# A spectral filter plus MLP on one core: the transform over d by half-sample cosines and sines

## The chip, the cores and the metric

The kernel runs on one core of a Trainium2 chip. A core has a matrix engine (TensorE, PE in the profile, with its weight loads as PEld), VectorE (DVE), ScalarE (ACT), GpSimd (POOL), SyncE (SP), which issues the DMAs here, and 16 DMA engines. The metric is device microseconds of one execution; the number given for a kernel is the median of several executions.

## What is computed

```python
xn = layernorm(x)                               # x: (1, 2048, 512), over the last axis
X  = rfft2(xn, axes=(-2, -1)) * (w_r + 1j*w_i)  # w: (2048, 257)
y  = irfft2(X, s=(2048, 512), axes=(-2, -1))
h  = xn @ w1 + b1                               # w1: (512, 1792)
out = x + y + (h * tanh(softplus(h))) @ w2      # w2: (1792, 512)
```

The two parts read the same normalised rows and are added. S = 2048 is the sequence, d = 512 the width.

## The kernel before, in words

Every matrix product is done in f16 with an operand split in a high and a low part: `mm3` (lines 59 to 65) issues three matmuls into one PSUM tile (high by high on line 61, high by low on line 64, low by high on line 65). Each result leaves PSUM as a new pair: ScalarE writes the high part, VectorE the low part (`split`, and lines such as 486 and 487).

**MLP.** For each of four groups of 512 rows and each of 14 blocks of 128 hidden units, `mlp_up` issues 12 matmuls into `ph`, ScalarE applies Mish into `hb`, and `split` makes the pair `a`; two blocks later `mlp_down` issues 12 matmuls into four accumulators `pa_0` to `pa_3`. These are all 128x512 matmuls, 1344 in all. A generator hands them out in half tiles of 12.

**Spectral part.** The sequence is written as 128 x 16, s = 16 s1 + s2.

- `s1_forward` (line 93): for each of 16 values of s2, three matmuls with the table cT against a row `xh` of 512 values of d, into `psS`; results go to DRAM (`d_y1`), to come back in another layout.
- `p2_unit` (line 332): the s2 transform, 16 tiles. d is cut in four quarters d2 of 128, and the 128x128 matrix `c_p2` acts on (part, s2, d2) at once: 16 s2 by 4 quarters by 2 parts. A tile `psP` is 12 matmuls 128 wide, and gives `z` with four planes k = 0..3.
- `spectrum` (line 358): once for each of four chunks c, the transform over the 128 values of d1 within a quarter, the weights, and the pair `u`. The even frequencies come first: `ere` and `eim` are six matmuls of 512 columns each, three for plane 0 and three for plane 1. ScalarE copies `eim` to `es`; VectorE forms four sums and differences X (lines 414 to 417), two products on VectorE and two on POOL with the weights `wE` (lines 421 to 424), two sums, four sums and differences back (lines 435 to 438), then the splits into planes 0 and 1 of `u`. For frequency 0 and the Nyquist column a row goes through `g0`, `r0`, `h0` by small DMAs, and in chunk 0 four columns are mended (lines 445 to 450). The odd frequencies follow: `ore` and `oim`, six matmuls each from planes 2 and 3, four products on VectorE straight from PSUM (lines 464 to 468), two sums on POOL, and the splits into planes 2 and 3 (the tiles `o` take the buffers of the `w`).
- `dp_unit` (line 476): the inverse over d1, 16 tiles `psA`. Planes 0 and 1 of `u` are added up into columns 0..255, planes 2 and 3 into 256..511: 12 matmuls of 256 columns. The pair `at` goes to DRAM (`d_a`).
- `ip_unit` (line 496): read back as `ai`, inverse over s2 with `c_ip2` into `psT`, pair `tt` to DRAM (`d_t`).
- `s1_inverse` (line 587): read back as `yi`, three matmuls of 512 columns into `psY`, added to the output rows.

**What sets the order.** `stream_a` (line 626) writes the spectral units for chunk c, those of chunk c - 1 and the pieces of `spectrum` between its `yield`s in turn, and the loop on line 699 lays MLP half tiles between them, up to half tile `B_END` = 100 in `N_UNITS` = 72 steps. A scheduler then sets the final order on each engine, and an engine works through its own list in that order. All spectral PSUM tiles share two buffers (`ps_f`, tag "f"); `u`, `z` and the `w` tiles have one buffer each.

Of the kernel before, what the change touches and what calls it, by code (L numbers as in the profile page):

```python
# [11 lines left out]
F16 = mybir.dt.float16  # L12
# [12 lines left out]
N_UNITS = 72  # L25
# [5 lines left out]
O_P2, O_IP2, O_DE, O_DO, O_IE, O_IO, O_ID = 0, 512, 1024, 2048, 3072, 4096, 5120  # L31
N_CM = 5120 + 128
# [3 lines left out]
def spectral_mlp_kernel(ctx, tc, x, wt, w0, w1, b1, w2, cT, cIT, cM, out):  # L36
# [36 lines left out]
    c_de = cMt[:, O_DE : O_DE + 1024].rearrange("p (e o h q) -> p e o h q", e=2, o=2, h=2)  # L73
    c_do = cMt[:, O_DO : O_DO + 1024].rearrange("p (e o h q) -> p e o h q", e=2, o=2, h=2)
    c_ie = cMt[:, O_IE : O_IE + 1024].rearrange("p (e h q) -> p e h q", e=2, h=2)
    c_io = cMt[:, O_IO : O_IO + 1024].rearrange("p (e h q) -> p e h q", e=2, h=2)
# [281 lines left out]
    def spectrum(c):  # L358
        s_u, c0t = sc["u"], sc["c0t"]
        z = zt[c]  # L360
        wEt, wOt = wts[c]
        u = tp.tile([P, 2, 4, 4, P], F16, tag="u", name=f"u_{c}")
        ut[c] = u

        def dmm(name, mat, k0, o):
            ps = ps_f.tile([P, 512], F32, tag="f", name=name)
            for e in range(2):
                mm3(
                    ps,
                    lambda h: mat[:, e, o, h, :],  # L370
                    lambda h: z[:, h, k0 + e].rearrange("p g q -> p (g q)"),
                    e == 0,
                    e == 1,
                    e == 0,
                )
            return ps

        def split_u(k, r):
            split(flat(u[:, 0, k]), flat(u[:, 1, k]), r, s_u)

        ere = dmm(f"ere_{c}", c_de, 0, 0)
        eim = dmm(f"eim_{c}", c_de, 0, 1)
        es = tp.tile([P, 512], F32, tag="xs", name=f"es_{c}", bufs=2)
        nc.scalar.copy(es, eim)

        er0 = tp.tile([1, 512], F32, tag="xs", name=f"er0_{c}", bufs=2)
        nc.scalar.copy(er0, ere[0:1, :])  # L387
        q0 = slice(32 * c, 32 * c + 4)
        g0 = sp.tile([P, 2, 2, 64], F32, tag="g0", name=f"g0_{c}")
        nc.sync.dma_start(  # L390
            g0[q0, 0].rearrange("g a q -> g (a q)"), er0.rearrange("p (g q) -> p g q", g=4)
        )
        nc.sync.dma_start(
# [62 lines left out]
        for h in range(2):  # L456
            for r in range(2):
                nc.sync.dma_start(u[0:1, h, r], h0[q0, h, r])
# [420 lines left out]
```

## Time and profile before

| | |
|---|---|
| median of 3 runs | 423.24 us (422.02 to 425.58) |
| profiled execution, first to last instruction | 424.4 us (no other time is recorded for it) |
| mean granted TensorE clock in it | 0.986 |
| busy: PE, PEld, DVE | 391.0, 194.1, 241.3 us |
| busy: ACT, POOL | 172.4, 42.2 us |
| matmuls | 2099 |
| DMA | 61.02 MB, mean 144 GB/s |

How to read the rows. A group has a line of the kernel, an engine, an operation, "out<-in" by the program's names, the shape and a count; behind the bar its busy time in us, the mean ns of one, and the idle time of the engine just before it with what ended it. A timeline row has its start and its length in us. A stretch has its length, then for PE, PEld, DVE, ACT and POOL the busy us with the number of instructions, then the granted clock, the busy share of the DMA engines and GB/s. In the chain of waits, each row is a piece of the work that ended last, followed back from the end.

### The profile page before, as it was taken

What the parts mean: (1) busy time and instruction counts of PE and PEld (TensorE: products, weight loads), DVE (VectorE), ACT (ScalarE), POOL (GpSimd) and SP (SyncE); (2) the same over time, 40 slices, a digit from 0 to 9 for tenths busy, and PEclk for the clock granted to TensorE, in tenths of its full rate; (3) what the DMA queues carried; (4) which work ended last, traced back from release to release, by engine and by line L of the source; (5) the groups of instructions that cost most, each with busy time, mean ns of one, the idle gap of its engine ahead of it and who ended that gap; (6) DMA issues with size and microseconds to landing.
All of it is one profiled execution on the core that took longest, in us unless ns stands there. A gap on an engine that the chain in (4) does not pass through costs nothing.

```text
span 424.4 us, 5542 instructions
## 1 busy us (share of the span) xinstructions
PE 391.0 (92%) x2099; PEld 194.1 (46%) x2099; DVE 241.3 (57%) x453; ACT 172.4 (41%) x261; POOL 42.2 (10%) x45
## 2 busy tenths in 40 slices
PE   0787899499899999989999999999999999999995
PEld 0433344244445455436554455554455544554442
DVE  5759899995455123773247943339625287332554
ACT  2896462442635324334343334333524243433110
POOL 0000102332040000220002020011200022000000
PEclk9999999889999999989999999999999999999999
DMA  7899882588154701032227214233024210233796
GB/s 247 268 345 330 272 259 91 159 256 269 53 160 114 233 25 51 0 99 71 81 76 239 85 49 123 76 127 124 2 74 151 74 51 25 76 127 126 219 296 247
DMA packets 48811, 61.02 MB, mean 144 GB/s; under 512 B 3168, under 2 KB 31360, under 8 KB 48528
## 3 DMA queue, kind: packets, MB, share of 16 engines
q1 hardware_dynamic: 48784, 60.67, 44.7%
q8 instruction: 16, 0.26, 0.2%
q14 instruction: 11, 0.09, 0.1%
HBM read 43.85 MB, written 16.78 MB: 143 GB/s over the span
## 4 chain that ended last, share of the span: by engine, by line
PE 72%; DVE 13%; DMA 6%; ACT 4%; issue 2%; POOL 0%; SPq 0%; DVEq 0%; ACTq 0%; POOLq 0%
PE pa L65 9%; PE pa L64 9%; PE pa L61 9%; PE ph L61 9%; PE ph L65 9%; PE ph L64 9%; DVE q L273 2%; DMA w1s<-in_w_dram 2%; PE pt L164 2%; ACT w1t L236 1%; PE psA L61 1%; PE psA L64 1%; PE psA L65 1%; DMA w2s<-in_w_dram 1%; DMA ai<-d_a 1%
## 5 line engine op out<-in xcount | busy, mean ns | idle before, releaser
L61 PE MATMUL ph<-xnT,w1t 128*128 128x512 f16 x224 | 85.2, 380 | 2.6 <-ACT hb L533 1.5
L533 ACT ACTIVATE hb<-ph,b1t,sc_exp 128x512 f32<-128x512 f32 x56 | 43.4, 775 | 107.4 <-PE ph L65 104.2
L65 PE MATMUL ph<-xnT,w1t 128*128 128x512 f16 x224 | 84.8, 379 | 2.4 <-DVE w1t L208 2.4
L61 PE MATMUL pa<-w2t,a 128*128 128x512 f16 x224 | 85.3, 383 | 1.6 <-ACT w2t L207 1.6
L64 PE MATMUL pa<-w2t,a 128*128 128x512 f16 x224 | 85.7, 383 | 0.3 <-DVE w2t L208 0.3
L65 PE MATMUL pa<-w2t,a 128*128 128x512 f16 x224 | 86.0, 384 | 0.0
L208 DVE SCALAR_TENSOR_TENSOR a<-hb,sc_a,a 128x512 f16<-128x512 f32 x56 | 42.3, 755 | 76.2 <-ACT a L207 76.1
L64 PE MATMUL ph<-xnT,w1t 128*128 128x512 f16 x224 | 85.0, 379 | 0.0
L207 ACT ACTIVATE a<-hb,sc_a 128x512 f16<-128x512 f32 x56 | 40.1, 719 | 2.2 <-PE pa L65 0.9
L65 PEld LDWEIGHTS <-w1t 128*128 128x128 f16 x224 | 21.9, 98 | 29.7 <-DVE w1t L208 3.4
L65 PEld LDWEIGHTS <-a 128*128 128x128 f16 x224 | 22.0, 98 | 27.4 <-issue 1.6
L64 PEld LDWEIGHTS <-w1t 128*128 128x128 f16 x224 | 21.9, 98 | 27.1 <-issue 2.3
L61 PEld LDWEIGHTS <-a 128*128 128x128 f16 x224 | 22.1, 99 | 26.5 <-issue 2.7
L61 PEld LDWEIGHTS <-w1t 128*128 128x128 f16 x224 | 21.9, 98 | 26.4 <-ACT w1t L207 1.6
L64 PEld LDWEIGHTS <-a 128*128 128x128 f16 x224 | 22.1, 99 | 25.2 <-issue 1.1
L164 PE MATMUL pt<-cMt,xh 128*128 128x128 f16 x128 | 12.3, 253 | 18.5 <-ACT xh L159 11.3
L487 DVE SCALAR_TENSOR_TENSOR at<-psA,at 128x512 f16<-128x512 f32 x16 | 11.0, 689 | 19.1 <-ACT at L486 19.1
L422 POOL TENSOR_TENSOR w<-X,wE 128x512 f32<-128x512 f32 x4 | 5.1, 1269 | 165.7 <-ACT er L387 76.8
L164 PEld LDWEIGHTS <-xh 128*128 128x128 f16 x128 | 10.3, 114 | 23.7 <-ACT xh L159 12.0
L509 DVE SCALAR_TENSOR_TENSOR tt<-psT,tt 128x512 f16<-128x512 f32 x16 | 11.0, 690 | 14.1 <-ACT tt L508 13.9
L160 POOL TENSOR_TENSOR xh<-xs,xh 128x512 f16<-128x512 f32 x12 | 14.4, 1216 | 45.2 <-ACT xh L159 29.9
L486 ACT ACTIVATE at<-psA 128x512 f16<-128x512 f32 x16 | 9.4, 589 | 22.8 <-PE psA L65 22.8
(150 smaller groups left out, 551.2 us busy)
## 6 DMA issues: line engine op xcount, KB each, us to landing
x<-in_x_dram SPq DMA_DIRECT2D x8, 512.0 KB
d_y<-y SPq DMA_DIRECT2D x8, 512.0 KB
wm<-in_wt_dram SPq DMA_DIRECT2D x8, 512.0 KB
yt<-d_y SPq DMA_DIRECT2D x16, 256.0 KB
d_a<-at SPq DMA_DIRECT2D x16, 256.0 KB
ai<-d_a SPq DMA_DIRECT2D x16, 256.0 KB
d_t<-tt SPq DMA_DIRECT2D x16, 256.0 KB
yi<-d_t SPq DMA_DIRECT2D x16, 256.0 KB
```

The costliest lines, as they stand in the source:

```text
L61: first = nc.tensor.matmul(ps, stat(0), mov(0), start=start, stop=False)
L64: nc.tensor.matmul(ps, stat(0), mov(1), start=False, stop=False)
L65: nc.tensor.matmul(ps, stat(1), mov(0), start=False, stop=stop)
L160: (nc.vector if g == 0 else nc.gpsimd).tensor_sub(xh[:, 1, :], xs, xh[:, 0, :])
L164: nc.tensor.transpose(pt[:, h, dc, :], xh[:, h, dc * P : (dc + 1) * P], ident)
L207: hi = nc.scalar.activation(dst_h, src, AF.Copy, scale=scale)
L208: nc.vector.scalar_tensor_tensor(dst_l, src, scale, dst_h, op0=ALU.mult, op1=ALU.subtract)
L273: nc.vector.tensor_reduce(q[:, c : c + 1], t, axis=AX.XY, op=ALU.max, apply_absolute_value=True)
L486: nc.scalar.mul(at[:, :, 0, :], ps, 2.0**-15)
L487: nc.vector.scalar_tensor_tensor(at[:, :, 1, :], ps, 2.0**-15, at[:, :, 0, :], op0=ALU.mult, op1=ALU.subtract)
L509: nc.vector.scalar_tensor_tensor(tt[:, :, 1, :], ps, 2.0**-12, tt[:, :, 0, :], op0=ALU.mult, op1=ALU.subtract)
L533: nc.scalar.activation(hb, ph, AF.Mish, bias=b1t[:, f : f + 1], scale=s_exp[k])
```

## The change

Before, the s2 matrices also carry two steps of an FFT over the quarters, and an output block over d1 is a sum over two planes. In the change, a row is laid out in four slots, with quarters 1 and 3 read backwards, so that position d1 counts outward from a fold and every sample stands half a step from it. The s2 matrices combine the four slots with signs only (matrix `e`), and each of the four planes k meets one 128x128 block: cosines and sines of (2 d1 + 1)(2 i + par) over 1024, par = 0 for even and 1 for odd frequencies. Its core:

```diff
-N_UNITS = 72
+N_UNITS = 76
...
-O_P2, O_IP2, O_DE, O_DO, O_IE, O_IO, O_ID = 0, 512, 1024, 2048, 3072, 4096, 5120
-N_CM = 5120 + 128
+O_P2, O_IP2, O_D, O_I, O_ID = 0, 512, 1024, 2048, 3072
+N_CM = 3072 + 128
...
     # s1_forward
-            mm3(ps, lambda h: cTt[:, s2, h, :], lambda h: xh[:, h, :], True, True)
+            psr = ps.rearrange("p (b a e) -> p a b e", b=2, a=2)
+            def slots(h, a):
+                v = xh[:, h, :].rearrange("p (b a e) -> p a b e", b=2, a=2)[:, a]
+                return v[:, :, ::-1] if a else v
+            for a in range(2):
+                mm3(psr[:, a], lambda h: cTt[:, s2, h, :], lambda h: slots(h, a), True, True)
...
-    def spectrum(c):
+    def spectrum(c, par):
...
+        k0 = 2 * par
-        def dmm(name, mat, k0, o):
+        def dmm(name, k):
             ps = ps_f.tile([P, 512], F32, tag="f", name=name)
-            for e in range(2):
-                mm3(ps, lambda h: mat[:, e, o, h, :],
-                    lambda h: z[:, h, k0 + e].rearrange("p g q -> p (g q)"), e == 0, e == 1, e == 0)
+            mm3(ps, lambda h: c_d[:, k, h, :], lambda h: z[:, h, k].rearrange("p g q -> p (g q)"), True, True, True)
...
     # dp_unit
-            for k, m in ((0, c_ie), (2, c_io)):
-                pk = flat(ps[:, k : k + 2])
-                for e in range(2):
-                    mm3(pk, lambda h: u[:, h, k + e, g, :], lambda h: m[:, e, h, :], e == 0, e == 1, k == 0 and e == 0)
+            for k in range(4):
+                mm3(ps[:, k], lambda h: u[:, h, k, g, :], lambda h: c_i[:, k, h, :], True, True, k == 0)
...
     # s1_inverse
-        mm3(ps, lambda h: sc["cIT"][:, s2, h, :], lambda h: yi[:, :, h, :], True, True, True)
+        psr = ps.rearrange("p (b a) e -> p a b e", a=2)
+        def slots(h, a):
+            v = yi[:, :, h, :].rearrange("p (b a) e -> p a b e", a=2)[:, a]
+            return v[:, :, ::-1] if a else v
+        for a in range(2):
+            mm3(psr[:, a], lambda h: sc["cIT"][:, s2, h, :], lambda h: slots(h, a), True, True, a == 0)
...
-                for wgt in spectrum(c):
-                    yield wgt
-                    if todo:
-                        ip_unit(*todo.pop(0))
-                        yield 0.8
+                for par in range(2):
+                    for wgt in spectrum(c, par):
+                        yield wgt
+                        if todo:
+                            ip_unit(*todo.pop(0))
+                            yield 0.8
```

`spectrum(c, 1)` replaces the odd half: `ore`, `oim`, the four products from PSUM and the two POOL sums are gone, and the odd half goes through the same copy, sums, products (with `wO`) and splits as the even half, without the `g0`, `r0`, `h0` part; in chunk 0 its four columns are mended too. `dre` and `dim` stand where `ere`, `eim` and `ore`, `oim` stood. The constant tables and the weight layout follow; the sizes of the weights do not change.

How the rows stand on the engines. Names end in a running number, and the second number in `dre_3` is the chunk, so both halves of a chunk read alike. The first place is VectorE in the odd half of the last chunk, c = 3. Before, from the first product of the odd half (line numbers of the kernel before):

```order
L464 TENSOR_TENSOR o_3_3280<-ore_3266,wO_2799 128x512
L208 SCALAR_TENSOR_TENSOR a_6_3263<-hb_6_3261,sc_a,a_6_3263 128x512
L465 TENSOR_TENSOR o_3_3282<-ore_3266,wO_2799 128x512
L467 TENSOR_TENSOR o_3_3281<-oim_3273,wO_2799 128x512
L468 TENSOR_TENSOR o_3_3283<-oim_3273,wO_2799 128x512
L208 SCALAR_TENSOR_TENSOR u_3107<-o_3_3280,sc_u,u_3107 128x512
L208 SCALAR_TENSOR_TENSOR u_3107<-o_3_3282,sc_u,u_3107 128x512
```

And now, from the last of the four sums and differences X (lines of the changed kernel):

```order
L419 TENSOR_TENSOR X_3_3307<-es_3_3305,dre_3_3297 128x256
L423 TENSOR_TENSOR w_1_3_3330<-X_3_3307,wO_2866 128x512
L425 TENSOR_TENSOR w_1_3_3331<-X_3_3307,wO_2866 128x512
L429 TENSOR_TENSOR w_1_3_3332<-w_1_3_3332,w_1_3_3333 128x512
L427 TENSOR_TENSOR w_1_3_3330<-w_1_3_3330,w_1_3_3331 128x512
L213 SCALAR_TENSOR_TENSOR a_6_3327<-hb_6_3325,sc_a,a_6_3327 128x512
L437 TENSOR_TENSOR w_1_3_3331<-w_1_3_3330 128x4x64
L438 TENSOR_TENSOR w_1_3_3333<-w_1_3_3330 128x4x64
L439 TENSOR_TENSOR w_1_3_3333<-w_1_3_3332 128x4x64
L440 TENSOR_TENSOR w_1_3_3331<-w_1_3_3332 128x4x64
L213 SCALAR_TENSOR_TENSOR u_3150<-w_1_3_3333,sc_u,u_3150 128x512
L213 SCALAR_TENSOR_TENSOR u_3150<-w_1_3_3331,sc_u,u_3150 128x512
```

Where seven instructions stood there are now fifteen with the first three X; the split of `a_6` moves from the second place to the ninth, and the last split of `u` is that of plane 2, from `w_1_3_3331`.

The second place is TensorE between the end of the odd half's transform and the first `psA` of the same chunk. Before, `oim` is followed by the down-projection of an earlier block and the up-projection `ph_7`, 12 matmuls each, and then by `psA`:

```order
L65 MATMUL oim_3273<-z_2801,cMt 128x512
L61 LDWEIGHTS a_4_3171
L61 MATMUL pa_0_3034<-w2t,a_4_3171 128x512
...
L65 MATMUL ph_7_3306<-xnT_1179,w1t 128x512
L61 LDWEIGHTS u_3107
L61 MATMUL psA_3324<-cMt,u_3107 128x256
```

Now `dim` is followed by `ph_6`, the down-projection and `ph_7`, again 12 matmuls each:

```order
L65 MATMUL dim_3_3301<-z_2868,cMt 128x512
L61 LDWEIGHTS w1t
L61 MATMUL ph_6_3312<-xnT_1215,w1t 128x512
...
L61 LDWEIGHTS a_4_3220
L61 MATMUL pa_0_3089<-w2t,a_4_3220 128x512
...
L65 MATMUL ph_7_3356<-xnT_1215,w1t 128x512
L61 LDWEIGHTS u_3150
L61 MATMUL psA_3378<-cMt,u_3150 128x128
```

So 36 matmuls 512 wide stand between them instead of 24. In chunks 0, 1 and 2 the number before the first `psA` is 43, 48 and 48, with one `psP` tile among them.

More of the change, by code (lines that the diff above doesn't have):

```diff
@@ L379, in split_u @@
             split(flat(u[:, 0, k]), flat(u[:, 1, k]), r, s_u)
[L381 to L392, printed above, removed]
@@ L402, in spectrum @@
[L402 to L407 removed]
+        dre = dmm(f"dre{par}_{c}", k0)
+        dim = dmm(f"dim{par}_{c}", k0 + 1)
+        es = tp.tile([P, 512], F32, tag="xs", name=f"es{par}_{c}", bufs=2)
```

172 lines of the change are left out of this document (61 added, 111 removed).

## The prediction

> **What bounds the kernel now.** I read the stretches of the span first, because the busy share of the page (PE 92%) is an average over stages with different limits. Busy time of each engine, then the granted TensorE clock and the DMA share:
>
> ```profile
> 120.00:180.00 60.00, 59.96 (x338) 29.57 (x337) 24.95 (x44) 23.63 (x37) 5.66 (x4) 1.00 0.30 93
> 180.00:200.00 20.00, 17.95 (x100) 8.97 (x99) 11.42 (x25) 8.08 (x12) 2.50 (x2) 0.91 0.22 67
> 200.00:360.00 160.00, 160.00 (x900) 82.55 (x899) 86.45 (x147) 60.48 (x94) 15.51 (x12) 1.00 0.29 93
> ...
> 380.00:420.00 40.00, 39.59 (x183) 17.55 (x181) 18.27 (x27) 7.21 (x11) 0.00 (x0) 1.00 0.67 216
> ```
>
> From 120 us on TensorE has no gap except in 180 to 200, while VectorE (third number) and ScalarE (fourth) have about half of their time free. A busy matmul row is not yet a matmul at its pace, so I read the pace from the starts in the timeline:
>
> ```profile
> 193.15 0.22 PE L61 MATMUL psP<-cMt,yt 128*128 128x128 f16 x1
> ...
> 193.82 0.27 PE L61 MATMUL psA<-cMt,u 128*128 128x256 f16 x1
> ...
> 195.13 0.38 PE L61 MATMUL ph<-xnT,w1t 128*128 128x512 f16 x1
> ...
> 197.72 0.22 PE L61 MATMUL psP<-cMt,yt 128*128 128x128 f16 x1
> ```
>
> Each step here is 12 matmuls. Twelve 128 wide take 193.82 - 193.15 = 0.67 us, twelve 256 wide 1.31, twelve 512 wide 2.59. So one costs 56, 109 or 216 ns: proportional to its width, back to back, and the 0.22 to 0.38 us in the second column is latency that overlaps. Whatever width is taken off TensorE in this stage comes off the span, as long as its inputs are ready. The end of the chain of waits confirms that nothing else sets the end: after the last spectral matmul stands a fixed tail of VectorE.
>
> ```profile
> 416.46 0.23 PE psY L65
> 416.72 1.33 DVE m L599 x2
> ...
> 420.10 0.66 DVEq L875
> ```
>
> **What the change removes.** The groups, one of three lines of each product:
>
> ```profile
> L61 PE MATMUL psA<-cMt,u 128*128 128x256 f16 x64 | 17.5, 273 | 0.0
> ...
> L61 PE MATMUL psY<-yi,cITt 128*128 128x512 f16 x16 | 6.1, 379 | 0.0
> ...
> L61 PE MATMUL ere<-z,cMt 128*128 128x512 f16 x8 | 3.0, 379 | 0.0
> ```
>
> Forward transform over d: ere, eim, ore, oim are 4 x 3 x 8 = 96 matmuls of 512; each output keeps three of its six, so 48 go: 48 x 0.216 = **-10.35 us**. Inverse over d: psA keeps its 192 matmuls (16 tiles of 12), at half the width; 16 x (1.31 - 0.67) = **-10.25 us**. The 128-wide row psP has the same form as the new psA, a fresh 128x128 weight for each matmul against a constant of cMt.
>
> [...]
>
> **What it adds on TensorE.** Each psS and psY tile becomes six matmuls of 256 for three of 512: 6 x 109 = 655 ns against 3 x 216 = 647, 8 ns by 32 tiles, **+0.2 us**. Half of them read their moving operand backwards, and no row of before has a negative step. Lower bound nothing; the row nearest in form, 256 wide with a positive step, gives 109 ns and I take it; the upper bound I set at two elements' time each, the row 512 wide. 48 of these lie in the inverse and 24 in the two last row groups of the forward stage, where TensorE is the bound: 72 x 0.109 = +7.9 us at that end.
>
> **What it adds on the chain of an odd half.** The second half of each spectrum used four VectorE products straight from PSUM, two POOL sums and two splits. It now runs the even half's chain: a ScalarE copy, four butterflies, two products on VectorE and two on POOL, two sums, four butterflies, two splits. The even half shows what that costs. From the last matmul of eim to its copy and the product tile after it:
>
> ```profile
> 339.73 0.38 PE L65 MATMUL eim<-z,cMt 128*128 128x512 f16 x1
> ...
> 361.96 0.27 PE L61 MATMUL psA<-cMt,u 128*128 128x256 f16 x1
> ```
> ```profile
> 340.15 0.58 ACT L384 COPY es<-eim 128x512 f32<-128x512 f32 x1 [4.47 <-PE eim L65]
> ...
> 352.13 0.72 ACT L207 ACTIVATE u<-w,sc_u 128x512 f16<-128x512 f32 x1 [2.15 <-DVE w L437]
> ```
> ```profile
> 227.16 0.42 DVE L414 TENSOR_TENSOR X<-ere,es 128x256 f32<-128x256 f32 x1
> ...
> 228.48 1.38 DVE L421 TENSOR_TENSOR w<-X,wE 128x512 f32<-128x512 f32 x1
> 229.78 1.75 DVE L423 TENSOR_TENSOR w<-X,wE 128x512 f32<-128x512 f32 x1
> ...
> 237.55 0.41 DVE L435 TENSOR_TENSOR w<-w 128x256 f32<-128x256 f32 x1
> ...
> 238.55 0.42 DVE L438 TENSOR_TENSOR w<-w 128x256 f32<-128x256 f32 x1
> ...
> 351.97 0.42 DVE L438 TENSOR_TENSOR w<-w 128x256 f32<-128x256 f32 x1
> 352.89 0.75 DVE L208 SCALAR_TENSOR_TENSOR u<-w,sc_u,u 128x512 f16<-128x512 f32 x1 [0.50 <-ACT u L207]
> 353.56 0.74 DVE L208 SCALAR_TENSOR_TENSOR a<-hb,sc_a,a 128x512 f16<-128x512 f32 x1
> ...
> 361.60 0.75 DVE L208 SCALAR_TENSOR_TENSOR u<-o,sc_u,u 128x512 f16<-128x512 f32 x1 [0.24 <-ACT u L207]
> ```
> ```profile
> L427 DVE TENSOR_TENSOR w<-w,w 128x512 f32<-128x512 f32 x4 | 2.8, 688 | 0.1
> ```
>
> Call T the start of the last dim matmul. Copy done at T + 0.42 + 0.58 = 1.0; butterflies 228.48 - 227.16 = 1.3, so 2.3; the two products, which stretch to 1.38 and 1.75 beside POOL where a sum of the same shape takes 0.69, end 229.78 + 1.75 - 228.48 = 3.05 later, 5.4; two sums at 0.65 to 0.69, 6.7; the up-projection's split a, which the new order puts between, 0.66, 7.4; the fourth butterfly starts 1.0 later, 8.4; the ScalarE split 0.16 after that, VectorE's 0.76 later, 9.3; a second pair, 0.67 + 0.75: the chain ends at **T + 10.7**.
>
> Against it stand the matmuls that the new order puts between dim and psA. In the last chunk these are 36 of 512: T + 37 x 0.216 = 8.0, and the ninth matmul of psA, the first that needs the later split, is due at 8 x 0.056 more, T + 8.4. It comes 2.3 us late, a little more because the even half's own split a and u stand in front of the first butterfly on VectorE. I take **+2.7 us**, bounds 0 and 3.7. Zero is possible: before, the last split started at 361.60, psA at 361.96, and TensorE did not stop. What is queued behind the wait on TensorE is pa and ph, so the MLP waits, and the psT reads that follow shift with it. In chunks 1 and 2, 48 matmuls and a psP tile lie between, T + 49 x 0.216 + 0.67 + 0.45 = 11.7, about one us of cover: I take **+0.5** for both, bounds 0 and 4.4 (2.2 each, as in the last chunk). In chunk 0 the fix-up columns lengthen the chain, but a wait that stands there already stays:
>
> ```profile
> 180.41 0.38 PE L64 MATMUL pa<-w2t,a 128*128 128x512 f16 x1
> 182.84 0.38 PE L61 MATMUL oim<-z,cMt 128*128 128x512 f16 x1 [2.05 <-DVE w L450]
> ...
> 183.91 0.53 PE L65 MATMUL oim<-z,cMt 128*128 128x512 f16 x1
> ...
> 187.54 0.38 PE L64 MATMUL pa<-w2t,a 128*128 128x512 f16 x1
> ```
>
> oim waits for ere's PSUM tile; the new dim waits for dre's in the same way. These rows also price what follows a wait: the nine starts after 183.91 take 3.63 us where nine at 0.216 take 1.94. The clock was halved for a while after a gap of only 2.2 us, and that cost 1.7. The halved clock also gives the odd chain of chunk 0 its missing time, so I put 0 there (bounds 0 and 1.7), and **+1.7** once, after the wait of the last chunk (bounds 0 and 1.7).
>
> [...] The rows here show the drop after 2.2 us, so I keep the term.
>
> **What it moves.** The constant load shrinks from 5120 to 3072 columns:
>
> ```profile
> 20.00:40.00 20.00, 15.50 (x69) 6.58 (x70) 15.17 (x28) 18.01 (x26) 0.46 (x1) 1.00 1.00 339
> ```
>
> cMt is issued in this stretch, where the DMA engines are full at 339 GB/s, ahead of the w2 loads; 128 x 2048 x 2 bytes are 0.52 MB or 1.5 us. VectorE is busy three quarters of the same time, so I take half, **-0.8** (bounds -1.5 and 0). The rest of the first 110 us only changes places, and its bounds are -1 and +1.
>
> Sum: -10.35 - 10.25 + 0.2 + 2.7 + 0.5 + 1.7 - 0.8 = -16.3. The profiled execution, 424.4 us, becomes 408.1. It stands 1.2 above the median of the runs, 423.24, so against the median I forecast **407 us**.
>
> **The rivals.**
>
> *Every wait is covered.* For it: the odd chain of before ended within half a us of psA, so the order is laid out closely. Against it: products beside POOL are more than twice as long as alone. Time: 423.2 - 10.35 - 10.25 + 0.2 - 0.8 = 402.
>
> *Every chunk waits.* If the odd chain starts 2 to 3 us late each time, because the even half is not yet off VectorE, chunks 1 and 2 pay what the last one pays, 2.2 + 1.7 each for the 0.5 I put: 407 + 7.3 = 414.3. Against it: about 1 us of cover more there.
>
> *Reversed reads run at half pace.* No row speaks for or against: 407 + 7.9 = 415.
>
> *Weight loads set the pace of 128-wide matmuls.* The groups have the load of one 128x128 weight:
>
> ```profile
> L61 PEld LDWEIGHTS <-a 128*128 128x128 f16 x224 | 22.1, 99 | 26.5 <-issue 2.7
> ```
>
> At 99 ns instead of 56, psA would cost 192 x 0.043 = 8.3 us more: 415. Against it: psP at 56 ns under loads of the same form. [...]
>
> *Slower: a reversed read costs several plain ones.* If a backward operand were fetched element by element at four times the time, 72 x 3 x 0.109 = 23.6 us would be added: 430.5. It decides from 16.3 / 72 = 0.23 us extra per matmul, three times the plain 0.109.
>
> *The gain is lost*, in the early stage or in waits not seen here, and the time stays within 1%.
>
> **How the numbers follow.** Chances: forecast 0.52; all covered 0.20; every chunk waits 0.12; half pace 0.07; loads 0.03; slower 0.03; lost 0.03. One per cent, 4.2 us, is about what a measurement of this kernel can tell from no change. The first five all lie more than that below 423.24: faster 0.94, same 0.03, slower 0.03. The range that leaves out two in ten reaches from the covered case, 402 less 1 for the early stage, to the third case: 401 to 414.
>
> **What would show it.** Right: psA at 56 ns a matmul; three matmuls in dre and dim; psY at 0.65 us a tile; a TensorE wait for ScalarE or VectorE at the first psA of the last chunk, 2 to 3 us, and matmuls at 0.43 us behind it; VectorE busier from 180 to 360. Wrong: psY or psS above 0.7 us a tile at full clock (the reversed reads), waits in chunks 1 and 2, or no wait at all.

## The result and the profile after

The changed kernel takes **410.01 us** (median of 4 runs, 408.26 to 412.07), the kernel before, run beside it, 424.41 (4 runs, 422.02 to 426.45). The ratio is 0.965, with a 95% interval from 0.960 to 0.970: 3.5% faster. The forecast was 407, range 401 to 414. The profiled execution of the change took 408.26 us, with a span of 406.5 from its first to its last instruction.

First the stretches, in the same columns as in the prediction (busy us of PE, PEld, DVE, ACT, POOL with counts, then clock, DMA share and GB/s):

```profile
120.00:180.00 60.00, 57.92 (x338) 29.65 (x337) 27.00 (x55) 23.62 (x36) 3.56 (x3) 1.00 0.28 87
180.00:200.00 20.00, 20.00 (x132) 10.59 (x131) 14.27 (x30) 8.47 (x14) 2.94 (x2) 0.93 0.31 95
200.00:340.00 140.00, 139.82 (x820) 70.43 (x819) 92.40 (x161) 59.66 (x94) 17.31 (x12) 1.00 0.32 102
340.00:360.00 20.00, 17.14 (x115) 8.91 (x114) 9.74 (x17) 7.81 (x12) 0.00 (x0) 1.00 0.29 93
```

From 200 to 340 TensorE still has no gap to speak of (139.82 of 140), and VectorE is busier, 92.40 / 140 = 0.66 against 86.45 / 160 = 0.54 before. A gap of 2.9 us has opened in 340 to 360. The groups of the changed products, one line of three each, and two starts that give the pace:

```profile
L61 PE MATMUL psA<-cMt,u 128*128 128x128 f16 x64 | 11.7, 219 | 2.0 <-ACT u L212 2.0
...
L61 PE MATMUL psY<-yi,cITt 128*128 128x256 f16 x32 | 8.7, 273 | 0.6 <-DMA yi<-d_t 0.6
...
L61 PE MATMUL dre<-z,cMt 128*128 128x512 f16 x8 | 3.0, 379 | 0.0
```
```profile
243.46 0.22 PE L61 MATMUL psA<-cMt,u 128*128 128x128 f16 x1
...
244.13 0.22 PE L61 MATMUL psP<-cMt,yt 128*128 128x128 f16 x1
```

A psA tile is 12 matmuls from 243.46 to 244.13, 0.67 us or 56 ns each. Next, what TensorE waits for behind 150 us, in total, number of waits, and the longest; first before, then after:

```profile
PE oim L61 <- DVE w L450: 2.1, 1, 2.1
PE psT L61 <- DMA ai<-d_a: 0.3, 1, 0.3
```
```profile
PE dim L61 <- DVE w L452: 2.1, 1, 2.1
PE psA L61 <- ACT u L212: 2.0, 1, 2.0
PE psT L61 <- DMA ai<-d_a: 0.7, 2, 0.5
PE psY L61 <- DMA yi<-d_t: 0.6, 1, 0.6
PE psA L65 <- DVE u L213: 0.6, 1, 0.6
PE dim L61 <- DVE at L473: 0.2, 1, 0.2
```

The wait in chunk 0 has stayed (oim is now dim). New are 2.6 us at the first psA of the last chunk, and behind it 1.3 at psT and psY, for data that come back from DRAM, where before had 0.3. The wait in the last chunk, on TensorE:

```profile
342.06 0.22 PE L61 MATMUL psA<-cMt,u 128*128 128x128 f16 x1
...
344.61 0.23 PE L61 MATMUL psA<-cMt,u 128*128 128x128 f16 x1 [2.05 <-ACT u L212]
344.68 0.22 PE L64 MATMUL psA<-cMt,u 128*128 128x128 f16 x1
345.45 0.23 PE L65 MATMUL psA<-cMt,u 128*128 128x128 f16 x1 [0.55 <-DVE u L213]
...
345.68 0.38 PE L61 MATMUL pa<-w2t,a 128*128 128x512 f16 x1
345.90 0.38 PE L64 MATMUL pa<-w2t,a 128*128 128x512 f16 x1
```

The tile takes 345.68 - 342.06 = 3.62 where 0.67 is normal: 2.95 us. The two pa behind it start 0.22 apart, so the clock is at full speed there. And the chain on ScalarE and VectorE that the tile waits for:

```profile
334.46 0.72 ACT L212 ACTIVATE a<-hb,sc_a 128x512 f16<-128x512 f32 x1
335.09 0.56 ACT L383 COPY es<-dim 128x512 f32<-128x512 f32 x1
...
335.88 0.42 DVE L416 TENSOR_TENSOR X<-dre,es 128x256 f32<-128x256 f32 x1
...
337.21 1.38 DVE L423 TENSOR_TENSOR w<-X,wO 128x512 f32<-128x512 f32 x1
...
338.51 1.75 DVE L425 TENSOR_TENSOR w<-X,wO 128x512 f32<-128x512 f32 x1
...
340.18 0.68 DVE L429 TENSOR_TENSOR w<-w,w 128x512 f32<-128x512 f32 x1
...
343.98 1.41 DVE L213 SCALAR_TENSOR_TENSOR u<-w,sc_u,u 128x512 f16<-128x512 f32 x2 [0.51 <-ACT u L212]
```

The last dim matmul starts at 334.07 (T), and the last split ends at 343.98 + 1.41 = 345.39, T + 11.3. The prediction had T + 10.7. The 0.6 arises at the front: ScalarE does a split `a` first, the copy starts 0.6 later than T + 0.42, and the first X at 335.88, T + 1.8, where the prediction had T + 1.0. From there on the chain is 0.2 shorter than priced.

**Where the time came from.** The two profiled executions, cut at two points of TensorE's timeline:

| | before | after | difference |
|---|---|---|---|
| start to the first psP | 155.50 | 153.14 | -2.4 |
| from there to the first psA of chunk 3 | 206.46 | 188.92 | -17.5 |
| from there to the end of the span | 62.44 | 64.44 | +2.0 |
| span | 424.4 | 406.5 | -17.9 |

The cut between the first two parts is at these rows, before and then after; the other is at the first psA of chunk 3 (361.96 and 342.06, shown above):

```profile
155.50 0.22 PE L61 MATMUL psP<-cMt,yt 128*128 128x128 f16 x1
```
```profile
153.14 0.22 PE L61 MATMUL psP<-cMt,yt 128*128 128x128 f16 x1
```

The middle part has 684 matmuls of the MLP in both kernels, and the last 180, so the cuts compare like with like. In the middle part all 48 matmuls of dre and dim go and 12 of the 16 psA tiles get shorter: -10.35 - 12 x 0.64 = -18.0, and 0.3 of small waits (dim of chunk 3, 0.18; one psA tile at 0.82) comes back: -17.7, within 0.2 us of the measured -17.5. In the last part TensorE has 2.4 us less work (-2.6 for four psA tiles, +0.2 for psY). Its starts fall 5.1 us behind their pace, 2.95 at psA and 2.2 at psT and psY, where before they fell 0.8 behind: -2.4 + 5.1 - 0.8 = +1.9, for the measured +2.0.

### The profile page after: what moved, and what is told of

Its sections match the earlier page's. It is cut to its first block, busy times and chain, and to the rows that moved or that the text cites. A ratio compares the mean times of both kernels' runs of the same rounds, so it can differ in the third digit from the quotient of the medians.

```text
span 406.5 us, 5681 instructions
## 1 busy us (share of the span) xinstructions
PE 370.0 (91%) x2147; PEld 190.1 (47%) x2147; DVE 256.7 (63%) x493; ACT 174.0 (43%) x265; POOL 42.8 (11%) x45
## 4 chain that ended last, share of the span: by engine, by line
PE 63%; DVE 18%; DMA 8%; ACT 6%; issue 3%; SPq 0%; POOL 0%; DVEq 0%; ACTq 0%; POOLq 0%
PE pa L65 8%; PE pa L64 8%; PE pa L61 8%; PE ph L65 8%; PE ph L64 8%; PE ph L61 8%; DVE a L213 2%; DMA w1s<-in_w_dram 2%; DMA w2m<-in_w_dram 2%; ACT w1t L241 2%; DMA ai<-d_a 1%; PE pt L169 1%; DMA d_a<-at 1%; DVE st L142 1%; DMA w2s<-in_w_dram 1%
## 5 line engine op out<-in xcount | busy, mean ns | idle before, releaser
L65 PEld LDWEIGHTS <-w1t 128*128 128x128 f16 x224 | 21.9, 98 | 29.3 <-DVE w1t L213 3.3
L64 PEld LDWEIGHTS <-w1t 128*128 128x128 f16 x224 | 21.9, 98 | 28.0 <-issue 4.0
L169 PE MATMUL pt<-cMt,xh 128*128 128x128 f16 x128 | 11.7, 241 | 17.9 <-ACT xh L164 11.1
L212 ACT ACTIVATE u<-w,sc_u 128x512 f16<-128x512 f32 x16 | 10.9, 714 | 23.6 <-DVE w L439 17.9
L165 POOL TENSOR_TENSOR xh<-xs,xh 128x512 f16<-128x512 f32 x12 | 14.4, 1218 | 45.9 <-ACT xh L164 31.6
L169 PEld LDWEIGHTS <-xh 128*128 128x128 f16 x128 | 9.7, 108 | 20.1 <-ACT xh L164 11.3
L495 DVE SCALAR_TENSOR_TENSOR tt<-psT,tt 128x512 f16<-128x512 f32 x16 | 11.0, 688 | 11.4 <-ACT tt L494 11.3
L494 ACT ACTIVATE tt<-psT 128x512 f16<-128x512 f32 x16 | 9.5, 596 | 20.0 <-PE psT L65 20.0
```

The lines of the kernel that those rows point to most:

```text
L64: nc.tensor.matmul(ps, stat(0), mov(1), start=False, stop=False)
L65: nc.tensor.matmul(ps, stat(1), mov(0), start=False, stop=stop)
L165: (nc.vector if g == 0 else nc.gpsimd).tensor_sub(xh[:, 1, :], xs, xh[:, 0, :])
L169: nc.tensor.transpose(pt[:, h, dc, :], xh[:, h, dc * P : (dc + 1) * P], ident)
L212: hi = nc.scalar.activation(dst_h, src, AF.Copy, scale=scale)
L494: nc.scalar.mul(tt[:, :, 0, :], ps, 2.0**-12)
```

## The experiments

Times are medians; each kernel is compared with the kernel before on its own chip. The first four, in five rounds, ran beside a kernel before at 425.9 us.

### The changed kernel once more

> The changed kernel once more, beside the others. Profile of the first run: TensorE waits 2.6 us (2.95 us longer than its pace) at the first psA of the last chunk, and the granted clock did not fall behind it, though it fell behind the 2.05 us wait in chunk 0; that run took 408.26 us, the fastest of four (up to 412.07). Theory: in most executions the clock does fall behind the last chunk's wait as well, and costs some 1.7 us; then this time is about 410 and a profile with a mean clock of 0.982 shows matmuls 0.43 us apart right behind psA. [...]

It took 410.05 (409.05 to 411.35), a ratio of 0.962 (0.960 to 0.965), with the same waits: 2.06 at dim of chunk 0, 2.05 and 0.55 at psA of chunk 3. Its profile (mean clock 0.986) shows half clock behind the wait at dim of chunk 0 and none behind psA of chunk 3, so it does not decide the question of the clock, to which the last experiment returns. This run is what the next three are held against.

### More matmuls ahead of the last chunk's psA

```diff
                     for wgt in spectrum(c, par):
                         ...
+                if c == 3:
+                    for _ in range(2):
+                        yield 0.0
```

Two empty steps let two more MLP pieces through: 60 matmuls instead of 36 between dim and psA.

> The changed kernel with two empty steps behind the last chunk's spectrum, so that 60 instead of 36 matmuls of 512 stand between dim and the first psA of that chunk; nothing else moves before it. Theory: the odd chain ended 11.3 us after the start of the last dim matmul (334.07 to 345.39), the cover is now 0.22 + 60 x 0.216 = 13.2 us, so the wait of 2.95 us goes, and with it the half clock behind it: 3 to 4.6 us faster than the changed kernel, about 406. Rival: the wait is only passed on to the psT reads and to psY behind it, since the DRAM round trips start no earlier: within 1 us of the changed kernel, waits at psT or psY larger by 2 to 3 us.

It took 412.18 (409.49 to 415.33), a ratio of 0.967 (0.963 to 0.972): not faster. It is 2.1 us above the repeat, more than the 1 us that the rival allowed, but its six runs lie 5.8 us apart. The wait at psA is gone in its profile, but these rows replace it, TensorE's waits from 340 us on:

```profile
PE psT L61 <- DMA ai<-d_a: 2.7, 3, 2.0
PE psY L61 <- DMA yi<-d_t: 2.1, 4, 0.8
```

4.8 us of waits for DRAM instead of 2.6 for the split of `u` and 1.3 for DRAM in the first profile of the change. The MLP pieces brought forward are the ones that covered the way psA, `d_a`, `ai`, psT, `d_t`, `yi`, psY. My theory, that this wait is a loss of its own, fell; the rival, that the end is one chain with too little cover (matmuls that TensorE can do meanwhile), held.

### The mended columns copied early

```diff
+        if c == 0:
+            dcol = sp.tile([P, 2], F32, tag="dcol", name=f"dcol_{par}", bufs=2)
+            nc.vector.tensor_copy(dcol, dre[:, 0:65:64])
...
-                    rre[:, j : j + 1], dre[:, j : j + 1], wre, m3[:, 0:1], op0=ALU.mult, op1=ALU.subtract
+                    rre[:, j : j + 1], dcol[:, a : a + 1], wre, m3[:, 0:1], op0=ALU.mult, op1=ALU.subtract
```

(and the same for `rim`). dre's PSUM tile is free sooner, and dim of the odd half no longer has to wait for line 452.

> The changed kernel with the two mended columns of dre copied out of PSUM early in chunk 0, so that dim of the odd half no longer waits for the mending. Theory: VectorE is the chain in this stretch. It is busy without a pause from 169 to 190, and the odd half's first butterfly at 181.04 follows its own even half directly. Taking the wait at dim away (2.2 us, and the 1.4 us of half clock behind it) brings dim forward but not the last split, so a wait of about 3 us appears at the first psA of chunk 0 instead: within 1 us of the changed kernel. Rival: the wait at dim is worth its own length, 3.6 us faster.

It took 412.58 (411.02 to 417.07), a ratio of 0.968 (0.965 to 0.971). The wait at dim went, and psA of the same chunk then waited 2.46, 0.50 and 0.16 us: VectorE's work for the two halves of chunk 0 is what is late, and the wait at dim was only the first place where it showed. The time is 2.5 us above the repeat, where it was expected within 1: the two profiles of this kernel (this one, of the slowest of its six runs, and one more below) have four and three windows at half clock between 88 us and the end of the matmuls, those of the change one each, and each such window, 3.41 us long, costs up to 1.7 us (512-wide matmuls start 0.43 us apart in it for 0.22).

### Both together

```diff
-                if c == 3:
+                if c in (0, 3):
                     for _ in range(2):
                         yield 0.0
```

The copies of the columns, and the empty steps behind chunks 0 and 3.

> The early copy, and two empty steps behind the spectrum of chunks 0 and 3: between dim and the first psA stand 60 matmuls of 512 in chunk 0 and 48 in chunks 1, 2 and 3. Theory: both waits and the half clock behind them go (2.2 + 1.4 in chunk 0, 2.95 and in most runs 1.7 in chunk 3; 0.3 us may be left in chunk 3 where the cover is 0.22 + 48 x 0.216 + 0.45 = 11.0 us against a chain of 11.3): 6 to 8 us faster than the changed kernel, 402 to 404. Rival: MLP tiles brought forward are missing at the end, psY waits for its reads there and gives the gain back: 406 or more.

It took 408.03 (407.32 to 409.78), a ratio of 0.958 (0.955 to 0.961): 2 us below the changed kernel, where 6 to 8 were hoped for. The waits at dim of chunk 0 and at psA of chunk 3 are gone; the first psA tile of chunk 0 still takes 1.87 us for 0.67, and psY waits 4.2 us for `yi` at the end. Moved cover helps in one place and is missing in another.

### psA at its old width

```diff
-            for k in range(4):
-                mm3(ps[:, k], lambda h: u[:, h, k, g, :], lambda h: c_i[:, k, h, :], True, True, k == 0)
+            for k0 in (0, 2):
+                pk = flat(ps[:, k0 : k0 + 2])
+                for e in range(2):
+                    mm3(pk, lambda h: u[:, h, k0 + e, g, :], lambda h: c_i[:, k0 : k0 + 2, h, :],
+                        e == 0, e == 1, k0 == 0 and e == 0)
```

> Each psA tile goes back to the two 128x128 blocks per output of before: 12 matmuls of 256 columns over a pair of planes, the wrong second plane being added in (the output is therefore not the reference's); all else, the quarter sums and the order included, stays as in the changed kernel. If the width alone pays, the psA tile goes from 0.67 to 1.31 us and the kernel loses 16 x 0.64 = 10.2 us, to about 420, less whatever the longer psA gives back as cover for the psT and psY waits at the end (up to 1.2 us): 9 to 10.3 slower than the changed kernel. If weight loads or waits set the pace of the stage, the loss is under 6 us. The wait at the first psA of chunk 3 should stand as it is, 2 to 2.6 us.

This and the next three ran in three rounds beside a kernel before at 425.41. It took 416.36 (415.73 to 417.07), a ratio of 0.979 (0.974 to 0.984): 5.7 above the forward-reading kernel below, which equals the changed one. So it is not 9 to 10.3, and it is under 6, but not for the reason named. The trace parts the two. First the starts in this kernel, then the first in the changed one, whose second is 342.06, shown above:

```profile
191.00 0.27 PE L61 MATMUL psA<-cMt,u 128*128 128x256 f16 x1
...
349.33 0.27 PE L61 MATMUL psA<-cMt,u 128*128 128x256 f16 x1
```
```profile
191.47 0.22 PE L61 MATMUL psA<-cMt,u 128*128 128x128 f16 x1
```

From the first psA of chunk 0 to that of chunk 3 there are 349.33 - 191.00 = 158.33 us, against 342.06 - 191.47 = 150.59: 7.74 more, 12 tiles at 0.645, the full price. At the end the tile of chunk 3 waits 0.97 + 0.45 instead of 2.05 + 0.55, psT 0.4 instead of 0.7, and psY not at all. The longer psA is cover itself, and by the starts of the matmuls 2.3 us of what it costs come back there. From the first psP to the end of the span this profile takes 261.3 us, those of the change and its repeat 253.4 and 253.2: some 8.0 us. Why the times differ by 5.7 only is not shown. The stage ahead of the first psP, which the edit does not touch, ends at 152.67 here and at 153.14 to 155.65 in the four profiles of the unchanged order, so it alone differs by up to 3 us.

### dre and dim with six matmuls

```diff
-            mm3(ps, lambda h: c_d[:, k, h, :], lambda h: z[:, h, k].rearrange("p g q -> p (g q)"), True, True, True)
+            for e in range(2):
+                mm3(ps, lambda h: c_d[:, k, h, :], lambda h: z[:, h, k0 + e].rearrange("p g q -> p (g q)"),
+                    e == 0, e == 1, e == 0)
```

> dre and dim take six matmuls of 512 each again, as in the kernel before (two planes are added up where one is wanted, so the output is not the reference's); all else stays. If each of the 48 matmuls taken away paid its 0.216 us, this kernel is 10.35 us slower than the changed one, about 420.4, or a little less, since the longer dim and dre give the chain of the halves more time and may cover the 2 us wait at dim of chunk 0 or part of the wait at psA of chunk 3: 7 to 10.4 slower. If the forward stage were bound by VectorE or by the transfers of yt, the loss would be under 5 us.

It took 418.66 (417.50 to 421.39), a ratio of 0.986 (0.980 to 0.991): 8.0 above the forward-reading kernel, within 7 to 10.4. Between the first psA of chunk 0 and that of chunk 3, 8.4 us are added, where 36 of the 48 matmuls make 7.8. As there, the wait in chunk 3 shrinks (1.29 + 0.55), by 0.8 us. The profile is that of the slowest of the four runs (421.39), and from the first psP to its end it is 10.8 us longer than the profile of the change, so nothing of the price of the 48 matmuls is given back there; where the difference to the 8.0 of the medians lies is not shown.

### Quarters read forwards

```diff
-                return v[:, :, ::-1] if a else v
+                return v
```

(in `s1_forward` and in `s1_inverse`)

> The two reversed quarters are read and written forwards (the columns land mirrored, so the output is not the reference's); nothing else differs. If a negative step costs nothing, the time is within 1 us of the changed kernel and psY and psS stay at 0.65 us per tile. If reversed reads were slow anywhere, on TensorE in psY and psS or on VectorE in the quarter sums, the kernel is faster by over 1 us: at half pace by 7.9 us.

It took 410.70 (410.43 to 411.25), a ratio of 0.966 (0.961 to 0.972): the same as the changed kernel. A moving operand read backwards costs nothing here. In the changed kernel the starts show it too, here in one psY tile of six matmuls, of which three read forwards and three backwards:

```profile
379.95 0.27 PE L61 MATMUL psY<-yi,cITt 128*128 128x256 f16 x1
...
380.28 0.27 PE L61 MATMUL psY<-yi,cITt 128*128 128x256 f16 x1
...
380.61 0.27 PE L61 MATMUL psY<-yi,cITt 128*128 128x256 f16 x1
```

The first three take 380.28 - 379.95 = 0.33 us and the last three 380.61 - 380.28 = 0.33, 109 ns each, as the old psA with its 256 columns.

### The odd half's products all on VectorE

```diff
-        nc.gpsimd.tensor_mul(flat(w_[2]), Xr, wP[:, 1])
+        (nc.vector if par else nc.gpsimd).tensor_mul(flat(w_[2]), Xr, wP[:, 1])
         nc.vector.tensor_mul(flat(w_[1]), Xi, wP[:, 1])
-        nc.gpsimd.tensor_mul(flat(w_[3]), Xi, wP[:, 0])
+        (nc.vector if par else nc.gpsimd).tensor_mul(flat(w_[3]), Xi, wP[:, 0])
```

> The odd half's two products that GpSimd did are done by VectorE, with the same output. Beside GpSimd, VectorE's own two products took 1.38 and 1.75 us; alone such a product takes 0.69. [...] If GpSimd's products cost VectorE nothing (the 1.38 and 1.75 being VectorE's own), the two extra ones add 1.4 us to the chain of each odd half: chunk 3 waits 1.4 longer, chunks 1 and 2 begin to wait, 1 to 4 us slower.

It took 408.26 (407.69 to 408.70), a ratio of 0.960 (0.956 to 0.965): 2.4 us below the forward-reading kernel on the same chip, where my estimate was within 1 us (four products alone, 4 x 0.69 = 2.8 us, for the 3.0 to 3.1 of the pair beside GpSimd): right in its sign and too timid. (The ratio alone does not part it from the repeat of the changed kernel on another chip, 0.962.) VectorE, doing twice the products, is done sooner. The four in chunk 3:

```profile
338.55 0.69 DVE L423 TENSOR_TENSOR w<-X,wO 128x512 f32<-128x512 f32 x1
339.16 0.69 DVE L424 TENSOR_TENSOR w<-X,wO 128x512 f32<-128x512 f32 x1
...
340.36 0.69 DVE L426 TENSOR_TENSOR w<-X,wO 128x512 f32<-128x512 f32 x1
```

The next operation starts at 340.96: 2.41 us for four, where the two beside GpSimd took 340.18 - 337.21 = 2.97. The chain ends at T + 10.7 instead of T + 11.3 (T is 335.42 here, and the last split ends at 346.13). More of the gain is the order: the scheduler now lays five pa matmuls inside the psA tile, and the stretch from the first psA of chunk 3 to the next tile, with the same 12 psA and 12 pa in it, takes 347.93 - 343.40 = 4.53 us instead of 348.27 - 342.06 = 6.21. From the first psP to the end of the span this profile takes 252.1 us, those of the change and its repeat, which have their half clock in the same place, 253.4 and 253.2. So 1.0 to 1.2 of the 2.4 us are located, and the rest is not.

### Both halves' products on VectorE

```diff
-        nc.gpsimd.tensor_mul(flat(w_[2]), Xr, wP[:, 1])
+        nc.vector.tensor_mul(flat(w_[2]), Xr, wP[:, 1])
...
-        nc.gpsimd.tensor_mul(flat(w_[3]), Xi, wP[:, 0])
+        nc.vector.tensor_mul(flat(w_[3]), Xi, wP[:, 0])
```

> Both halves' products, even and odd, are all done by VectorE; GpSimd does none; same output. If VectorE and GpSimd hold each other up (a product takes 0.69 us alone on VectorE, and beside GpSimd 0.89 to 1.75), the pair of engines gains nothing by sharing: VectorE's total busy time stays within 5 us of the changed kernel's 256.7 although it has 16 products of 0.69 more, the even half's products take 2.5 us for 2.8 or so, and the time is that of the kernel with only the odd half moved, a ratio to before of 0.960, within 0.004. If the sharing does save VectorE time in the even half (rival), VectorE is over 5 us busier, the chunk waits grow, and the ratio is above 0.964.

Five rounds beside a kernel before at 424.48: **405.41** (404.75 to 406.95), a ratio of 0.957 (0.953 to 0.961). No run of it is as slow as the fastest of the changed kernel, though by the ratio the kernel with both together above (0.958) is as good. VectorE's groups of products in the changed kernel:

```profile
L425 DVE TENSOR_TENSOR w<-X,wO 128x512 f32<-128x512 f32 x4 | 7.0, 1749 | 0.0
...
L423 DVE TENSOR_TENSOR w<-X,wO 128x512 f32<-128x512 f32 x4 | 5.5, 1374 | 0.0
...
L425 DVE TENSOR_TENSOR w<-X,wE 128x512 f32<-128x512 f32 x4 | 4.9, 1223 | 0.1
...
L423 DVE TENSOR_TENSOR w<-X,wE 128x512 f32<-128x512 f32 x4 | 3.6, 889 | 0.0
```

and, in this one, the same line 425 among eight groups that all look alike:

```profile
L425 DVE TENSOR_TENSOR w<-X,wE 128x512 f32<-128x512 f32 x4 | 2.7, 687 | 0.1
```

VectorE spent 7.0 + 5.5 + 4.9 + 3.6 = 21.0 us on 16 products with GpSimd doing the other 16; alone it does all 32 in 8 x 2.74 = 21.9. Its busy time is 254.2 us in all, against 256.7. The sharing saved nothing, and it made each half's chain longer. How, GpSimd's two products in chunk 3 of the changed kernel show:

```profile
336.76 1.27 POOL L424 TENSOR_TENSOR w<-X,wO 128x512 f32<-128x512 f32 x1 [11.39 <-issue]
337.99 1.72 POOL L426 TENSOR_TENSOR w<-X,wO 128x512 f32<-128x512 f32 x1
```

They end at 338.03 and 339.71. VectorE's two, which started meanwhile (337.21 and 338.51, shown above), end at 338.59 and 340.26, each 0.55 to 0.56 us after GpSimd's, about what a product takes alone from start to start (0.60). In the profile after, all 13 products of VectorE that started while one of GpSimd ran ended 0.54 to 0.56 us behind it: here the two engines worked one after the other, and why is not shown. Where no product of GpSimd ran at the time, one of VectorE took 0.69 us in the changed kernel too (even half, starts at 224.58, 225.68 and 326.17); the means of 889 and 1223 ns mix the two cases.

The wait at dim of chunk 0 falls from 2.05 to 0.56, that at psA of chunk 3 from 2.6 to 0.39. From the first psP to the end of the span the profile takes 249.1 us, 4.1 to 4.3 less than the change and its repeat; no window is at half clock behind 88 us any more, which is 1.7 of it. The order on TensorE changed as well (39 matmuls 512 wide instead of 43 between dim and the first psA of chunk 0, and seven more inside that tile), and what the products are worth by themselves is not parted from that.

### All of it, with the end kept covered

```diff
-N_UNITS = 76
+N_UNITS = 80
```

With it the products on VectorE, the columns copied early, and the two empty steps behind chunks 0 and 3.

> All products on VectorE, the two mended columns of dre copied early in chunk 0, two empty steps behind the spectrum of chunks 0 and 3, and the MLP half tiles spread over 80 steps where the changed kernel has 76, so that 48 matmuls stand before the first psA of chunk 3 and the end keeps the half tiles that it has in the changed kernel. If the waits are what is left to gain and the end is held by its transfers only where half tiles are missing, the wait at dim of chunk 0 (2.05) and those at psA of chunk 3 (2.6) go and none comes at psY: 4 to 6 us off 410.4, a ratio of 0.951 to 0.956. If the waits only move (the rival that the first pair of experiments bore out), psY or psT waits for over 2 us at the end and the ratio is 0.958 or more.

It took 405.99 (404.26 to 408.37), a ratio of 0.958 (0.954 to 0.962), against 0.951 to 0.956 hoped for; it is where the rival had it. The waits at dim of chunk 0 and at psA are gone; psT waits 1.9 and psY 1.8 for DRAM. Once the chains are short, more cover gains nothing: 405.41 with the plain order is as good.

### When does the clock fall?

The prediction put 1.7 us of half clock behind the wait of the last chunk. The profile after shows none there, though it shows some behind a wait of the same 2.05 us at dim of chunk 0. I laid the edges of the granted clock of all profiles side by side. In each, every edge lies a whole number of 3.413 us behind the first: after, 80.57, 83.98, 179.56 and 182.97 are 0, 1, 29 and 30 steps (102.40 / 30 = 3.413). So I cut the timeline on that grid. The changed kernel, two windows at dim of chunk 0 and three at psA of chunk 3:

```profile
176.14:179.55 3.41, 1.36 (x7) 0.49 (x6) 3.38 (x14) 1.41 (x3) 0.00 (x0) 1.00 0.00 0
179.55:182.96 3.41, 3.41 (x10) 1.21 (x8) 3.40 (x8) 1.33 (x3) 1.04 (x1) 0.50 0.54 156
...
339.97:343.39 3.42, 2.59 (x17) 1.24 (x15) 3.42 (x8) 0.17 (x1) 0.00 (x0) 1.00 0.00 0
343.39:346.80 3.41, 1.64 (x12) 0.88 (x13) 2.28 (x5) 3.06 (x5) 0.00 (x0) 1.00 0.00 0
346.80:350.21 3.41, 3.41 (x26) 1.91 (x25) 1.00 (x2) 0.60 (x1) 0.00 (x0) 1.00 0.27 77
```

TensorE is idle for 3.41 - 1.36 = 2.05 in one window, and the next is at half clock (0.50). In chunk 3 the grid cuts the pause in 0.83 and 1.77, and nothing follows. Over the 12 profiles, from 88 us to the end of the matmuls, no window at full clock with up to 1.77 us of idle time was followed by half clock, and all with 2.05 or more were; one with 1.85 was. Ahead of 88 us the border is as blurred: 1.91 and 1.95 us idle were followed by half clock (from 75.04 in the kernel with both together, from 74.80 in the repeat), and 2.02 in the profile after (from 32.78) was not. Two more executions put this to the test.

> The changed kernel as it is, one more execution, to test a rule read from the 12 profiles so far: the granted clock changes only on a grid of 3.413 us that stands anywhere against the kernel, and a window of the grid in which TensorE was idle for more than 1.86 us is followed by one at half clock, a window with 1.76 us or less is not. By the rule every edge lies a whole number of 3.413 us behind the first, and the pause of 2.05 at dim of chunk 0 and those of 2.05 and 0.55 at psA of chunk 3 cost 1.7 us behind them only where one window holds over 1.86 of them. If instead the length of a single pause decides (the rival), the 2.05 at dim and the 2.05 at psA have the same consequence.

> The kernel with the two columns of dre copied early, one more execution, for the same rule of the clock. It has three larger pauses: at psA of chunk 0 (2.46, 0.50, 0.16), at psA of chunk 3 (2.05 and 0.6), and one near 110 us in the forward stage. Expected by the rule: each edge on the 3.413 us grid, and half clock behind exactly the windows with over 1.86 us of idle time. By the rival, half clock behind every pause of 2.05 or more, wherever the grid lies.

One execution each: 411.87 and 413.21 us, the kernel before beside them 422.75. All edges lay on the grid. In the changed kernel it was the other way round this time:

```profile
176.98:180.40 3.42, 2.66 (x13) 0.99 (x11) 3.42 (x11) 1.50 (x2) 0.00 (x0) 1.00 0.00 0
180.40:183.81 3.41, 2.11 (x10) 1.00 (x11) 3.37 (x11) 1.80 (x3) 0.00 (x0) 1.00 0.33 67
344.24:347.66 3.42, 0.82 (x10) 0.47 (x9) 2.79 (x7) 2.25 (x4) 0.00 (x0) 1.00 0.00 0
347.66:351.07 3.41, 3.41 (x12) 1.49 (x13) 1.39 (x2) 1.06 (x2) 0.00 (x0) 0.50 0.16 47
```

The 2.06 at dim are cut in 0.76 and 1.31 and cost nothing more; the pause at psA lies in one window, 2.60 idle, and the next window is at half clock. In the other kernel the windows with 2.46 and 2.26 idle were followed by half clock, and no other that was at full clock behind 88 us. One thing the rule had left out: the window behind the 2.46, itself at half clock and 0.66 idle, was followed by a second one at half clock. The rival, that the length of a single pause decides, is refuted: the same pause cost 1.7 us in one place in one execution, and in the other place in the next.

## Why the prediction was right, point by point

- **Forward matmuls, -10.35.** Right on TensorE: the middle part of the span has them at full price. Put back, they cost 8.0 us by the medians and 10.8 behind the first psP in the one profile; the difference is not explained.
- **psA, -10.25.** The term was right on TensorE (0.67 for 1.31 us per tile, 7.74 for 12 of the 16 tiles), but some 8.0 of it reach the span behind the first psP, because narrower tiles expose 2.3 us of waits at the end; the medians differ by 5.7, and the rest of that is not located.
- **psS and psY in halves, +0.2, reversed reads at nothing.** Right: six of 256 columns take 0.65 to 0.66 us, and reading forwards changes nothing. The rivals of half pace and of four times the cost are refuted.
- **Weight loads as the pace.** Refuted by the psA rows of the profile after, 56 ns with a fresh weight each.
- **Wait of the last chunk, +2.7.** Measured 2.95. The two products (2.97 us for 3.05) and the splits came as priced; the chain ended 0.6 later than T + 10.7 because the copy and the first X came late, which the prediction names as a little more without a number.
- **Chunks 1 and 2, +0.5.** Nearly nothing: the first psA tile of chunk 2 takes 0.82 for 0.67, as its ninth matmul (293.43) comes just behind the last split of `u` (292.6 + 0.75 = 293.35); with chunk 3's dim that is 0.3. The last dim matmul of chunk 2 starts at 281.60, so the chain ends at T + 11.75 there, and the about one us of extra cover was all used up. The case in which every chunk waits is refuted.
- **Chunk 0, 0.** Right: the wait at dim stayed, and psA had none in this execution; where no half clock fell behind dim, it showed waits of 0.5 and 0.32.
- **Half clock, +1.7.** Mis-sized. Of four profiles of this order it fell behind chunk 3's wait in two (reading forwards, and the execution for the clock), and in the other two (the change, its repeat) behind dim of chunk 0, where before had one too. So each has one such window, as before has. With it at dim the stretch from the first psP to the end takes 253.4 and 253.2 us, with it behind chunk 3 254.4 and 254.2, so the term is worth nothing in two of the four and about 1.0 in the other two. In these four its place went with where the grid fell.
- **Load of cMt and early stage, -0.8.** -2.4 in the one pair of profiles. The first psP starts between 152.67 and 155.65 us in the kernels that do not touch that stage, apart from one profile at 158.46, and before's 155.50 lies among them; one profile of before is too little to say what the smaller load is worth. This stays open.
- **The sum.** It came out 16.3 below the time before; measured are 14.4 (424.41 to 410.01) and, in the longer series, 15.9 (425.9 to 410.05). The term that is missing is the one that I named in half a sentence, that the psT reads shift with the wait, and gave no price: psT and psY wait 1.0 us more than before by the marked waits, 1.4 by the starts. It is partly luck that the sum fits: the 1.7 of half clock that were counted and did not come in the profile after stand against these 1.4 that were not counted. From the first psP on the forecast had 16.3 - 0.8 = 15.5 us, and the profile has 17.5 - 2.0 = 15.5. Of the 3 us between 407 and 410, 1.2 are the base: the median of the three runs shown was 423.24, and the four runs beside the change have 424.41. The other 1.9 are gain that is missing in this series (14.4 for 16.3); in the longer one, whose base is 425.9, only 0.4 is missing. That I set a span, 424.4, beside a median of times, which are 1.75 us longer than their spans, was a mistake too, though it left the forecast where it was, since the sum is taken off the median either way.

The list of what would show it right was met, but for the matmuls at 0.43 us behind the wait of the last chunk, which the profile after does not have; the one with quarters read forwards has them.

## What to carry to other kernels

When TensorE's work shrinks, price the wait and also what stands behind it in the same chain: here cover moved ahead of one wait was missing at the next. Covering the last wait alone and freeing dim alone paid nothing (0.967 and 0.968 for the change's 0.962); covering both waits (0.958) and taking the shared products out of the chain (0.957) each paid about as much, and all of it together no more (0.958). An engine that "takes half" of an elementwise step is worth looking up in the rows: if its partner's operations get longer by as much, as here (21.0 us of VectorE for 16 products beside GpSimd, 21.9 for all 32 alone), the split is no help, and the chain is shorter without it. A pause had no fixed price in clock here: the same 2.05 us cost 1.7 more or nothing.

## What the runs showed of the hardware

- In all 14 profiles the granted TensorE clock changed on a grid of 3.413 us (after: 30 steps from 80.57 to 182.97). It did not lie alike against the kernel: the wait at dim of chunk 0 fell in one window in the profile after (2.05 idle) and was cut in 0.76 and 1.31 in the execution for the clock. From 88 us to the end of the matmuls every window at full clock with 2.05 us or more of idle time was followed by one at half clock, where 512-wide matmuls start 0.43 us apart for 0.22 (after, from 179.66), up to 1.7 us lost; none with up to 1.77 was, and between lie one window at 1.85 with (dre and dim with six matmuls, from 353.01), and one at 1.86, in the tail of the kernel with all products on VectorE (from 397.44), without. Ahead of 88 us 1.91 (both together, from 75.04) and 1.95 (the repeat, from 74.80) went with a fall and 2.02 (after, from 32.78) without. What it takes to come back is less clear: windows at half clock with 0.60 (columns copied early, from 196.19) and 0.66 idle (the same kernel once more, from 191.82) were followed by a second one, others with 0.65 (after, from 80.57) and 0.78 (the repeat, from 81.63) were not.
- A product w<-X,wO of 128x512 f32 took 0.69 us alone on VectorE (338.55 to 340.36 in the kernel with the odd half's products there). Beside a product of GpSimd it took, in the profile after, 0.77 where it overlapped that one by 0.2 us (w<-X,wE, at 272.09), and up to 1.76 where it had to wait for most of one (at 272.78); GpSimd's own took 1.26 to 1.72.
- A 128-wide matmul with a fresh 128x128 weight took 56 ns (12 in 0.67 us, psA in the profile after), and a moving operand with a step of -1 cost nothing (three 256-wide matmuls in 0.33 us, as forwards; 410.70 us with all read forwards for 410.01).
